# Attention, mixture of experts and gated layer in one kernel: row sums on ScalarE's accumulator, two jobs moved to GpSimd, fewer filler matmuls

## The chip, the cores and the metric

The kernel runs on one core of a Trainium2 chip. A core has five engines that run side by side and wait for each other through semaphores: TensorE (PE in the rows, with its weight loads as PEld), VectorE (DVE), ScalarE (ACT), GpSimd (POOL) and SyncE (SP), which issues most of the DMA transfers. The metric is the time of one execution in microseconds (us); lower is better.

## The reference

Three stages follow each other. The inputs q, k and v are float32 of shape (2, 8, 576, 64).

```python
# 1. attention, per batch and head, scale = 1/8, factor = 4
q_d, k_d, v_d = (mean over groups of 4 positions of q, k, v)      # 144 coarse positions
out_d = softmax(scale * q_d @ k_d.T) @ v_d, each row repeated 4 times
out_local = softmax(scale * q @ k.T where |i - j| < 4, else -1e9) @ v
x = (out_up + out_local) as 1152 tokens x 512
# each softmax: a = exp(s - max); a = a / (sum(a) + 1e-9)
# 2. experts: P from x @ w_gate by 8 rounds of row and column scaling
out = sum over e < 8 of P[:, e] * (relu(x @ w1[e]) @ w2[e])       # 512 -> 1024 -> 512
# 3. gated layer on that result: ((x @ w_a) * (x @ w_b)) @ w_out  # 512 -> 1536 -> 512
```

## The kernel before

Matrix products run on operands that are split into a high and a low part, both in a 32-bit format (fp32r in the rows): high times high, high times low and low times high are added up in PSUM. For weights the helper `split` does this: ScalarE casts the raw tile to its high part (line 134), and an engine of choice, VectorE if none is named, subtracts to get the low part (line 135).

The attention is cut into 24 items, one for each batch, pair of heads and third of the sequence (192 queries in three chunks of 64). An item goes through small stages, and the generator `side` runs them as a software pipeline: in each of its rounds `s` it issues, for five items at once, `a1` (TensorE transposes q, and k where the item is the first of its heads), `b1` (TensorE: mask, local scores, coarse scores of the item before), `c3` (ScalarE copies local weights out of PSUM), `a2` (ScalarE copies of kT and of q), `b4` (row sums, reciprocals, scaling of the exponentials), `d3` (splits the finished item into xh and xl), `b2` (VectorE: maxima), `a3` (VectorE: coarse keys and queries); then, after a yield, `d1` (TensorE: weights times v), `d2a`, `b3` (ScalarE: the exponentials), `c1` (TensorE transposes the weights), `d2`, `c2` and, for items that are the first of their heads, `sum_vd` (GpSimd sums v over groups of four, lines 865 and 868); then it yields again. "Round" below is such a pass. In the trace a round is taken from one mask matmul of `b1` to the next: 12.45, 16.64, 20.07, 24.99, 28.43, 33.40, 37.34, 42.34 and 45.85 us.

Every engine works through its own queue in the order in which the kernel is written, so that an instruction that waits holds all behind it on that engine. The order is set by hand and by the Python code that calls the generator. The main loop cuts the 1152 tokens into three blocks of 384. Ahead of block 0 it only steps through `side` until the tokens of that block are there, which takes 23 half rounds:

```python
while ready[0] < b:
    side_step()
    if b == 0:
        warm(WARM[1])
    nside += 1
    if nside > 12 and nside % 2 == 0:
        run_first(1)
```

`warm(n)` issues n bfloat16 matmuls of 256 columns whose results nobody reads; 16 more stand at the program's start. `run_first(1)` runs the next prepared weight job, here a call of `split`. Blocks 0, 1 and 2 then compute the first two halves of expert 0 (`g_plain` for the first layer, `o_moe` for the second), and between their groups of matmuls `step` goes on with the attention of the later items. From about 165 us on, the rest (experts and gated layer) runs with another order, which a planner in Python sets: the class `Model` adds up estimated times of TensorE, VectorE, ScalarE and GpSimd, and jobs are placed where these estimates let them.

What the change and the steps of the prediction touch: `queue_plain` (lines 235 to 245) prepares the first layer's weights of a unit in four pieces, i = 0, 1 and j = 0, 1, in the order (0,0), (0,1), (1,0), (1,1); j names one of two raw tiles, each of which is given back to the loading queue after its second piece. `a3` reduces the keys over groups of four (line 909), multiplies by 1/16 (line 912), and reduces the queries (line 914). `b3` takes exponentials chunk by chunk (line 950) and the coarse ones with a sum from ScalarE's accumulator (line 953). `b4` sums the local ones (line 961), adds 1e-9 (962), takes reciprocals (963), and scales the local weights on GpSimd (964) and the coarse ones on VectorE (967). The names in the rows: `p` and `pd` are local and coarse weights, `rsum` and `rr` row sums and reciprocals, `kd` coarse keys, `qdbd` coarse queries, `rv`, `rawv` and `vd` v before and after the sum over four, `pdT` and `plT` transposed weights, `raw` a raw weight tile, `w` a split one, `wz` and `identb` operands of the filler matmuls.

Of the kernel before, what the change touches and what calls it, by code (L numbers as in the profile page):

```python
# [12 lines left out]
AF = mybir.ActivationFunctionType  # L13
ALU = mybir.AluOpType
AX = mybir.AxisListType
# [4 lines left out]
def attn_moe_glu_kernel(  # L20
# [16 lines left out]
    nc = tc.nc  # L37
# [12 lines left out]
    NC = UT // 64  # L50
    W = 70
# [42 lines left out]
    def dve(us, after=None):  # L94
        M.dve = max(M.dve, M.pe if after is None else after) + us

    def act(us):
        M.act = max(M.act, M.pe) + us
# [20 lines left out]
    def new_block(uses):  # L119
        i = nring[0] % NSLOT  # L120
        assert RING[i] is None or RING[i].uses == 0
        nring[0] += 1
        t = wr.tile([128, 1024], F32R, tag=f"w{i}", name=f"w{i}")
        RING[i] = Block(t[:, 0:512], t[:, 512:1024], uses)
        return RING[i]

    def pool(us):
        M.pool = max(M.pool, M.pe) + us

    def split(b, raw, k=1, low=None):  # L130
        hi, lo = b.hi, b.lo
        if k > 1:
            hi, lo = (t.rearrange("p (k f) -> p k f", k=k) for t in (hi, lo))
        nc.scalar.copy(out=hi, in_=raw)  # L134
        (low or nc.vector).tensor_tensor(out=lo, in0=raw, in1=hi.bitcast(F32), op=ALU.subtract)  # L135
        act(0.6)
        if low is None:
            dve(0.75, 0.0)
        else:
            pool(1.35)  # L140
# [88 lines left out]
    def halves(load, left):  # L229

        rs = [Raw(lambda t, j=j: load(t, j), left[j]) for j in range(len(left))]
        lq.extend(rs)
        return rs

    def queue_plain(u, uses=6):

        u.w = {}
        rs = halves(u.load1, (2, 2))
        for i in range(2):
            for j in range(2):  # L240
                def piece(i=i, j=j):
                    b = u.w[i, j] = new_block(uses)
                    split(b, rs[j].tile[:, :, 256 * i:256 * i + 256], 2)
                    rs[j].used()
                wq.append(Task(piece, 0.68, ready=rs[j].ready, slot=True))

# [166 lines left out]
    for e in range(E):  # L413
        for hf in range(2):
            u = Unit()
# [7 lines left out]
    for g in range(GU):  # L423
        u = Unit()
# [481 lines left out]
    def a3(i, b, u, hp):  # L906
        if u == 0:
            kd_ = at.tile([128, SD], F32, tag=f"kd{hp}", name=f"kd{hp}", bufs=1)
            nc.vector.tensor_reduce(
                out=kd_, in_=kT[b, hp].rearrange("p (t r) -> p t r", r=4), axis=AX.X, op=ALU.add  # L910
            )
            nc.vector.tensor_scalar_mul(out=kd_, in0=kd_, scalar1=1.0 / 16.0)
            kd[b, hp] = kd_
        nc.vector.tensor_reduce(
            out=qdbd[i % 2].rearrange("p c h t -> p (c h t)"),
            in_=qbd[i % 2].rearrange("p c h (t r) -> p (c h t) r", r=4), axis=AX.X, op=ALU.add,
        )
# [26 lines left out]
    def b3(i, b, u, hp):  # L944
        sl, sd, nm, nd = pB[i]
        p = at.tile([128, NC, W], F32, tag="p", name="p", bufs=2)
        pd = at.tile([R, SD], F32, tag="pd", name="pd", bufs=2)
        rs = rsum[i % 4]
        for c in range(NC):
            nc.scalar.activation(  # L950
                out=p[:, c], in_=sl[:, c * W:(c + 1) * W], func=AF.Exp, bias=nm[:, c:c + 1], scale=1.0
            )
        nc.scalar.activation(
            out=pd, in_=sd, func=AF.Exp, bias=nd, scale=1.0, accum_out=rs[0:R, NC:NC + 1],
        )
        pB[i] = p, pd, rs

    def b4(i, b, u, hp):
        p, pd, rs = pB[i]
        rr = at.tile([128, NC + 1], F32, tag="rr", name="rr", bufs=2)  # L960
        nc.vector.tensor_reduce(out=rs[:, 0:NC], in_=p, axis=AX.X, op=ALU.add)
        nc.vector.tensor_scalar_add(out=rr, in0=rs, scalar1=1e-9)
        nc.vector.reciprocal(out=rr, in_=rr)  # L963
        nc.gpsimd.tensor_tensor(  # L964
            out=p, in0=p, in1=rr[:, 0:NC].unsqueeze(2).to_broadcast([128, NC, W]), op=ALU.mult
        )
        nc.vector.tensor_scalar_mul(out=pd, in0=pd, scalar1=rr[0:R, NC:NC + 1])
        pB[i] = p, pd
# [134 lines left out]
    def side():  # L1103
# [7 lines left out]
        for s in range(n + 5):  # L1111
# [14 lines left out]
            do(c3, s - 3)  # L1126
            do(a2, s)
            do(b4, s - 2)
            do(d3, s - 4)
            do(b2, s - 1)  # L1130
            do(a3, s)
            yield
            do(d1, s - 3)
            do(d2a, s - 3)
            do(b3, s - 1)
            do(c1, s - 2)
            do(d2, s - 3)
# [20 lines left out]
        )  # L1158


    WARM = (16, 3)
    SIDE = 1.25

    def warm(n):

        if n:
            ps = bank("g")
            for _ in range(n):
                mm(ps[:, :256], identb, wz, True, True)

    with tc.manual_schedule():
# [4 lines left out]
        nc.vector.memset(wz, 1.0)  # L1176
        warm(WARM[0])
        make_identity(nc, ident)
# [8 lines left out]
        for h in range(2):  # L1187
            ph = slice(64 * h, 64 * h + 64)
            for base, cm, st_ in ((9, 1, -1), (-3, -1, 1)):
                nc.gpsimd.affine_select(  # L1190
                    out=mw[ph], in_=mw[ph], compare_op=ALU.is_ge, fill=-1e30, base=base,
# [6 lines left out]


        for u in units[:2]:  # L1200
            queue_plain(u)
        for u in units[:2]:
            queue_out(u)
        queue_combined(units[2], nc.gpsimd)
# [26 lines left out]
        def close_attention():  # L1231
            nonlocal closed, ps3, Th, Tl, tmp_p
            closed = True
            attn_stack.close()
            tp = ctx.enter_context(tc.tile_pool(name="tp", bufs=1, side="right"))
            Th = tp.tile([128, 3, 2, S], F32R, name="Th")
            Tl = tp.tile([128, 3, 2, S], F32R, name="Tl")
            for x in range(3):
                G3.append([tp.tile([128, 320], F32, name=f"G{x}{fi}") for fi in range(2)])
            tmp_p = tmp_stack.enter_context(tc.tile_pool(name="tmp", bufs=1, side="right"))  # L1240
            ps3 = ctx.enter_context(tc.tile_pool(name="ps3", bufs=6, space=PSUM))
            gens[0] = gating()
            v, g = nc.vector, nc.gpsimd
            tasks = combine_x(0, lambda name: tmp_p.tile([128, 2, CN[0]], F32, name=name),
                              (v, g, g, v), (g, g, g, g))
            tq.extend(tasks)
            queue_out(units[2])
            for u in units[3:]:
                queue_combined(u)
                queue_out(u)  # L1250
            for u in glu_g:
                if u is glu_g[0]:
                    queue_plain(u, 8)
                else:
                    queue_combined(u)
                queue_out(u, 2)
            hold[0] = False
            for r in coming:
                r.tile
            fetch()  # L1260
# [36 lines left out]
        for b in range(NB):  # L1297
# [5 lines that stand above are left out]
# [155 lines left out]
```

## Time and profile before

| | us |
|---|---|
| median of three runs | 1093.15 (1090.24 to 1093.36) |
| profiled execution, whole | 1091.71 |
| profiled execution, span of its instructions | 1089.8 |
| TensorE busy in the span | 1076.0 |
| VectorE, ScalarE, GpSimd busy | 790.8, 456.8, 515.5 |

The span runs from the first to the last instruction; 1.9 us of the execution lie outside it. Times within the trace count from the span's start. Busy time counts an engine as busy from an instruction's start to its end, and the ends of matmuls are modelled. In rows of the timeline, a row gives start, duration, engine, line, operation, output and inputs, sizes, the count of merged instructions, and in brackets how long the engine sat idle before and who released it. The chain of waits is the path that ended last, followed backwards.

### The profile page before, as it was taken

The numbers are of one execution on the slowest core, as the hardware profiler recorded it, in microseconds if no ns is written. First come the engines' busy times: TensorE is split into PE (matmuls) and PEld (weight loads), VectorE is DVE, ScalarE is ACT, GpSimd is POOL, SyncE is SP. The second block draws the span as 40 slices with busy tenths as digits, with TensorE's granted clock in tenths as the row PEclk, the third lists the DMA queues.
The fourth block names the chain that finished last, engine by engine and source line by source line (L and its number), as shares of the span: only waits on it lengthen the run. The fifth ranks groups of instructions, "written<-read, shape, count | busy, mean of one in ns | idle before, by whom it ended". The sixth has DMA issues, their size and how long they took to land.

```text
span 1089.8 us, 18094 instructions
## 1 busy us (share of the span) xinstructions
PE 1076.0 (99%) x6569; PEld 974.5 (89%) x6569; DVE 790.8 (73%) x1545; ACT 456.8 (42%) x1135; POOL 515.5 (47%) x512
## 2 busy tenths in 40 slices
PE   9999999999999999999999999999999999999998
PEld 8898988999898989889898988989999899999997
DVE  7876546857887788878777888877864576677764
ACT  5664424454434443343444344344443453232221
POOL 3324116563645556464565646455561365355521
PEclk9999999999999999999999999999999999999999
DMA  7453000213323132332323233231311101111002
GB/s 173 124 144 88 22 5 17 91 47 98 102 85 103 63 124 73 113 101 85 102 64 124 62 122 101 86 102 63 110 65 49 49 1 59 58 43 56 20 21 87
DMA packets 80745, 84.52 MB, mean 78 GB/s; under 512 B 35856, under 2 KB 54288, under 8 KB 80656
## 3 DMA queue, kind: packets, MB, share of 16 engines
q1 hardware_dynamic: 79472, 83.07, 24.8%
q8 instruction: 52, 0.85, 0.3%
q10 hardware_dynamic: 1184, 0.30, 0.1%
q14 instruction: 37, 0.30, 0.1%
HBM read 71.54 MB, written 11.80 MB: 76 GB/s over the span
## 4 chain that ended last, share of the span: by engine, by line
PE 75%; DVE 13%; ACT 5%; issue 3%; DMA 2%; POOL 1%; DVEq 0%; ACTq 0%; SPq 0%; POOLq 0%
PE g L60 70%; PE at L60 3%; DVE w L135 3%; DVE G L652 2%; DVE acc L513 2%; ACT w L134 1%; ACT G L644 1%; DVE dec L374 1%; DVE dec L357 1%; DVE dec L352 1%; ACT gh L646 1%; POOL gl L648 1%; DVE gl L638 1%; DMA dec<-in_moe_w_a_dram 1%; DMA dec<-in_moe_w_b_dram 1%
## 5 line engine op out<-in xcount | busy, mean ns | idle before, releaser
L60 PE MATMUL g<-w,gh 128*128 128x512 f32 x1314 | 412.9, 395 | 0.3 <-DVE acc L513 0.3
L60 PE MATMUL g<-xh,w 128*128 128x256 f32 (+2 forms) x1536 | 339.1, 302 | 0.3 <-DVE lg L1053 0.3
L648 POOL TENSOR_TENSOR gl<-G,gh 128x256 fp32r<-128x256 f32 (+1 forms) x208 | 172.1, 836 | 269.4 <-ACT gh L646 262.9
L60 PEld LDWEIGHTS g<-w,gh 128*128 128x128 f32 x1314 | 235.7, 188 | 41.8 <-DVE acc L513 1.4
L60 PEld LDWEIGHTS g<-xh,w 128*128 128x128 f32 x1536 | 257.5, 189 | 4.7 <-DVE lg L1053 0.4
L60 PE MATMUL g<-w,gl 128*128 128x512 f32 x657 | 257.8, 392 | 0.0
L60 PE MATMUL g<-xl,w 128*128 128x320 f32 (+2 forms) x768 | 231.2, 301 | 1.5 <-POOL xl L1030 1.5
L135 DVE TENSOR_TENSOR w<-raw,w 128x512 fp32r<-128x512 f32 x139 | 137.4, 998 | 112.8 <-ACT w L134 112.6
L60 PE MATMUL g<-Th,w 128*128 128x320 f32 (+1 forms) x912 | 199.7, 295 | 1.6 <-DVE G L652 1.6
L652 DVE TENSOR_TENSOR G<-g,G 128x256 f32<-128x256 f32 (+1 forms) x380 | 154.9, 448 | 21.4 <-PE g L60 10.1
L60 PEld LDWEIGHTS g<-Th,w 128*128 128x128 f32 x912 | 152.2, 188 | 7.2 <-DVE G L652 4.3
L644 ACT ACTIVATE G<-G 128x256 f32<-128x256 f32 (+1 forms) x168 | 74.3, 443 | 192.6 <-DVE G L652 192.6
L60 PEld LDWEIGHTS g<-xl,w 128*128 128x128 f32 x768 | 145.3, 189 | 6.2 <-POOL xl L1030 2.1
L60 PEld LDWEIGHTS g<-w,gl 128*128 128x128 f32 x657 | 123.4, 188 | 28.6
L60 PE MATMUL g<-Tl,w 128*128 128x256 f32 (+1 forms) x456 | 134.0, 294 | 0.0
L134 ACT CAST w<-raw 128x512 fp32r<-128x512 f32 x180 | 107.5, 618 | 52.4 <-POOL raw L259 46.2
L646 ACT CAST gh<-G 128x256 fp32r<-128x256 f32 (+1 forms) x208 | 90.3, 434 | 92.1 <-DVE G L662 78.6
L513 DVE SCALAR_TENSOR_TENSOR acc<-g,P,acc 128x512 f32<-128x512 f32 x126 | 93.7, 744 | 47.8 <-PE g L60 44.0
L389 POOL TENSOR_TENSOR dec<-dec 128x384 f32<-128x384 f32 x48 | 48.8, 1016 | 105.5 <-DVE dec L386 59.2
L60 PEld LDWEIGHTS g<-Tl,w 128*128 128x128 f32 x456 | 85.8, 188 | 2.8
L964 POOL TENSOR_TENSOR p<-p,rr 128x210 f32<-128x210 f32 x24 | 13.2, 551 | 107.1 <-DVE rr L963 29.9
L259 POOL TENSOR_TENSOR s<-raw 128x512 f32<-128x512 f32 x38 | 61.8, 1626 | 4.3 <-DMA raw<-w 3.8
(177 smaller groups left out, 1198.3 us busy)
## 6 DMA issues: line engine op xcount, KB each, us to landing
raw<-in_moe_w_dram SPq DMA_DIRECT2D x128, 256.0 KB
w<-dec SPq DMA_DIRECT2D x48, 192.0 KB
dec<-in_moe_w_a_dram SPq DMA_DIRECT2D x16, 384.0 KB
dec<-in_moe_w_b_dram SPq DMA_DIRECT2D x16, 384.0 KB
dec<-in_moe_w_out_dram SPq DMA_DIRECT2D x16, 384.0 KB
raw<-w SPq DMA_DIRECT2D x48, 128.0 KB
raw<-w SPq DMA_DIRECT2D x12, 256.0 KB
vw<-in_v_dram SPq DMA_DIRECT2D x72, 35.0 KB
```

Source lines behind the costliest of these rows:

```text
L60: nc.tensor.matmul(out=o, lhsT=l, rhs=r, start=start, stop=stop, skip_group_check=not check)
L134: nc.scalar.copy(out=hi, in_=raw)
L135: (low or nc.vector).tensor_tensor(out=lo, in0=raw, in1=hi.bitcast(F32), op=ALU.subtract)
L259: nc.gpsimd.tensor_tensor(out=o(), in0=A(*a), in1=A(*b), op=op)
L352: nc.vector.tensor_scalar(out=m.bitcast(F32), in0=m.bitcast(F32), scalar1=2.0**-15, scalar2=122879.9921875, op0=ALU.max, op1=ALU.min,)
L389: nc.gpsimd.tensor_tensor(out=tf, in0=tf, in1=mf, op=ALU.add)
L513: nc.vector.scalar_tensor_tensor(out=a, in0=ps, scalar=P[:, tt, u.e:u.e + 1], in1=a, op0=ALU.mult, op1=ALU.add)
L644: nc.scalar.activation(out=src, in_=src, func=AF.Relu)
L646: nc.scalar.copy(out=h, in_=src)
L648: nc.gpsimd.tensor_tensor(out=l, in0=src, in1=h.bitcast(F32), op=ALU.subtract)
L652: nc.vector.tensor_tensor(out=o, in0=bank_, in1=b, op=ALU.add)
L964: nc.gpsimd.tensor_tensor(out=p, in0=p, in1=rr[:, 0:NC].unsqueeze(2).to_broadcast([128, NC, W]), op=ALU.mult)
```

## The change

The sum over the local exponentials moves from a reduction on VectorE to the accumulator output of the three exponentials on ScalarE. The multiplication of the coarse keys by 1/16 moves from VectorE to GpSimd. Of the first layer's weights of the first two units, the low parts of the pieces with j = 1 (four pieces of eight) move from VectorE to GpSimd. The second number of `WARM` goes from 3 to 1.

```diff
-    def queue_plain(u, uses=6):
+    def queue_plain(u, uses=6, low=None):
...
-                    split(b, rs[j].tile[:, :, 256 * i:256 * i + 256], 2)
+                    split(b, rs[j].tile[:, :, 256 * i:256 * i + 256], 2, low if j else None)
...
-            nc.vector.tensor_scalar_mul(out=kd_, in0=kd_, scalar1=1.0 / 16.0)
+            nc.gpsimd.tensor_scalar_mul(out=kd_, in0=kd_, scalar1=1.0 / 16.0)
...
             nc.scalar.activation(
-                out=p[:, c], in_=sl[:, c * W:(c + 1) * W], func=AF.Exp, bias=nm[:, c:c + 1], scale=1.0
+                out=p[:, c], in_=sl[:, c * W:(c + 1) * W], func=AF.Exp, bias=nm[:, c:c + 1], scale=1.0,
+                accum_out=rs[:, c:c + 1],
             )
...
-        nc.vector.tensor_reduce(out=rs[:, 0:NC], in_=p, axis=AX.X, op=ALU.add)
...
-    WARM = (16, 3)
+    WARM = (16, 1)
...
-            queue_plain(u)
+            queue_plain(u, 6, nc.gpsimd)
```

Counted over the program, VectorE has 36 instructions fewer (24 sums, 8 factors, 4 low parts), GpSimd 12 more, TensorE 46 filler matmuls with their weight loads fewer; ScalarE's 72 local exponentials get a second output; SyncE's queue is unchanged. But for these the order on every engine is the same from the first instruction to the last, also where the planner sets it.

On VectorE, in the round of 20.07 us and the start of the next, the queue before read (`kd` coarse keys, `x` the finished item, `rsum` the row sums):

```order
L909 TENSOR_REDUCE kd_452<-kT_435 128x144
L912 TENSOR_SCALAR kd_452<-kd_452 128x144
L914 TENSOR_REDUCE qdbd_113<-qbd_111 128x96
L1019 TENSOR_TENSOR x<-at,od 64x192 x2
L986 COPY pdT<-at 72x192
L961 TENSOR_REDUCE rsum_118<-p 128x3
L962 TENSOR_SCALAR rr<-rsum_118 128x4
L963 RECIPROCAL rr<-rr 128x4
L967 TENSOR_SCALAR pd<-pd,rr 96x144
```

The same stretch on VectorE with the change:

```order
L909 TENSOR_REDUCE kd_433<-kT_417 128x144
L914 TENSOR_REDUCE qdbd_113<-qbd_111 128x96
L1019 TENSOR_TENSOR x<-at,od 64x192 x2
L986 COPY pdT<-at 72x192
L962 TENSOR_SCALAR rr<-rsum_118 128x4
L963 RECIPROCAL rr<-rr 128x4
L967 TENSOR_SCALAR pd<-pd,rr 96x144
```

The factor has left the place between the two reductions, and the sum the place ahead of the reciprocals. On GpSimd, from the round of 28.43 us to that of 37.34 us, the queue before read:

```order
L865 TENSOR_TENSOR rv_415<-rv_415 72x4x128
L868 TENSOR_TENSOR vd_640<-rv_415 72x2x2x64
L964 TENSOR_TENSOR p<-p,rr 128x210
L1030 TENSOR_TENSOR xl<-x,xh 128x192
L964 TENSOR_TENSOR p<-p,rr 128x210
L1030 TENSOR_TENSOR xl<-x,xh 128x192
L865 TENSOR_TENSOR rv_569<-rv_569 72x4x128
```

The two pairs of lines 964 and 1030 belong to two rounds. With the change the same stretch on GpSimd reads:

```order
L912 TENSOR_SCALAR kd_577<-kd_577 128x144
L865 TENSOR_TENSOR rv_397<-rv_397 72x4x128
L868 TENSOR_TENSOR vd_609<-rv_397 72x2x2x64
L964 TENSOR_TENSOR p<-p,rr 128x210
L1030 TENSOR_TENSOR xl<-x,xh 128x192
L135 TENSOR_TENSOR w_679<-raw,w_679 128x512
L964 TENSOR_TENSOR p<-p,rr 128x210
L1030 TENSOR_TENSOR xl<-x,xh 128x192
L865 TENSOR_TENSOR rv_541<-rv_541 72x4x128
```

The factor now stands ahead of the sums of v, and the low part of piece (0,1) ahead of the next round's scaling of `p`.

## Rows read from the trace of the kernel before

**Rows 1.** Busy time by stretch: us, then PE, PEld, DVE, ACT, POOL.

```profile
12.45:45.85 33.40, 31.46 (x276) 28.71 (x275) 30.53 (x89) 23.81 (x91) 16.14 (x25) 1.00 0.65 166
16.64:20.07 3.43, 3.43 (x34) 3.35 (x33) 3.16 (x9) 2.51 (x10) 2.08 (x3) 1.00 0.78 217
20.07:24.99 4.92, 4.62 (x41) 3.98 (x40) 4.58 (x15) 3.20 (x14) 2.12 (x4) 1.00 0.79 167
50.20:1089.80 1039.60, 1030.56 (x6196) 934.09 (x6196) 748.42 (x1413) 424.66 (x1020) 494.99 (x473) 1.00 0.23 74
```

**Rows 2.** Chain of waits: start us, us, what.

```profile
24.16 0.33 PE g L60 x3
```

**Rows 3.** Timeline 17.8 to 22.1: start, us, engine, line.

```profile
17.84 0.55 POOL L964 TENSOR_TENSOR p<-p,rr 128x210 f32<-128x210 f32 x1 [2.76 <-PE at L60]
...
19.09 1.27 POOL L865 TENSOR_TENSOR rv<-rv 72x512 f32<-72x512 f32 x1
...
19.19 1.27 DVE L912 TENSOR_SCALAR kd<-kd 128x144 f32<-128x144 f32 x1
...
20.44 0.72 POOL L868 TENSOR_TENSOR vd<-rv 72x256 f32<-72x256 f32 x1
...
22.08 0.66 PE L60 MATMUL at<-pdT,vd 72*128 72x96 f32 x4 [0.30 <-DVE pdT L986]
```

**Rows 4.** Line 912, all eight: ns min/median/max.

```profile
L912 DVE TENSOR_SCALAR kd<-kd x8: 234/808/1295, 7.2 to 83.5; 128x144 f32<-128x144 f32 x8
```

**Rows 5.** Timeline, ACT after an exponential with a sum.

```profile
10.08 0.20 ACT L953 ACTIVATION_READ_ACCUMULATOR pd<-at,nd 96x1 f32 x1
10.17 0.40 ACT L897 COPY kT<-at 128x288 f32<-128x288 f32 x1
```

**Rows 6.** Timeline 33.6 to 36.0: first low part's round.

```profile
33.67 0.62 ACT L134 CAST w<-raw 128x512 fp32r<-128x512 f32 x1
...
34.93 0.37 DVE L961 TENSOR_REDUCE rsum<-p 128x3 f32<-128x210 f32 x1
...
35.33 0.17 DVE L962 TENSOR_SCALAR rr<-rsum 128x4 f32<-128x4 f32 x1
...
35.88 0.55 POOL L964 TENSOR_TENSOR p<-p,rr 128x210 f32<-128x210 f32 x1 [2.83 <-PE at L60]
```

**Rows 7.** Line 135 up to 180 us, on DVE and POOL.

```profile
L135 DVE TENSOR_TENSOR w<-raw,w x13: 677/692/694, 30.4 to 79.4; 128x512 fp32r<-128x512 f32 x13
...
L135 POOL TENSOR_TENSOR w<-raw,w x1: 1280/1280/1280, 176.1 to 176.1; 128x512 fp32r<-128x512 f32 x1
```

**Rows 8.** Timeline 38.2 to 39.6: DVE and POOL meeting.

```profile
38.26 0.69 DVE L135 TENSOR_TENSOR w<-raw,w 128x512 fp32r<-128x512 f32 x1 [0.24 <-ACT w L134]
38.29 1.24 POOL L868 TENSOR_TENSOR vd<-rv 72x256 f32<-72x256 f32 x1
...
39.27 0.29 DVE L962 TENSOR_SCALAR rr<-rsum 128x4 f32<-128x4 f32 x1
39.48 0.21 POOL L1155 CAST wgp<-wg 128x32 fp32r<-128x32 f32 x1
...
39.59 0.69 PE L60 MATMUL at<-pdT,vd 72*128 72x96 f32 x4 [0.76 <-POOL vd L868]
```

**Rows 9.** Timeline 28 to 33: TensorE waiting for the coarse weights.

```profile
32.25 0.36 PE L975 MATMUL at<-ident,pd 96*72 96x96 f32 x2 [0.40 <-DVE pd L967]
```

**Rows 10.** Timeline, TensorE at the start.

```profile
1.32 3.57 PE L60 MATMUL g<-wz,identb 128*128 128x256 bf16 x16 [1.32 <-DVE wz L1176]
...
4.69 0.52 PE L880 MATMUL at<-ident,qn 96*128 96x96 f32 x2
...
8.97 0.33 PE L880 MATMUL at<-ident,qn 96*128 96x96 f32 x2
```

**Rows 11.** Timeline, TensorE at the first block.

```profile
47.10 0.42 PE L60 MATMUL g<-xh,w 128*128 128x384 f32 x1
...
50.20 0.44 PE L60 MATMUL g<-xl,w 128*128 128x384 f32 x1 [1.11 <-POOL xl L1030]
```

## The prediction

> **What bounds the kernel now.** I read four views: the page's busy times, then the busy times of stretches, then the chain of waits over the first 190 us, then the timeline of the rounds. The page's 1076.0 us of TensorE in a span of 1089.8 say that little but TensorE matters for most of the program. The stretches sharpen this: from 50.20 us on TensorE is busy for 1030.56 of 1039.60 us [rows 1], and everything that the change touches beyond that point lies beside running matmuls. What can move the time are the first 47 us, ahead of block 0, whose first matmul starts at 47.10 [rows 11] and which needs what the attention's rounds compute.
>
> Take the eight rounds from 12.45 to 45.85 us. TensorE is busy for 31.46 of 33.40 us, so 1.94 us idle, and VectorE for 30.53 [rows 1]: two engines near their limit. In the round from 16.64 to 20.07 TensorE has no gap (3.43 of 3.43) [rows 1]; this is what a round costs when only TensorE's own queue counts, with two sets of three filler matmuls in it. Three of these stand in the chain with 0.33 us, 0.11 each [rows 2]. The round from 20.07 to 24.99 is longer, with 0.30 us of idle TensorE, and its story is told by VectorE and GpSimd: GpSimd starts the sum of v at 19.09 for 1.27 us; VectorE starts the factor of the coarse keys 0.10 us later, and that too takes 1.27 us and ends 0.10 us after GpSimd's instruction [rows 3]. The same instruction takes 0.234 us where it is not held, and up to 1.295 us over its eight instances [rows 4]. So VectorE is held by GpSimd there, and everything behind it with it.
>
> **Filler matmuls.** 23 places lose two matmuls each: 46 x 0.11 = 5.1 us of TensorE. They pay only where TensorE's queue is what the next stage waits for. Both of a round's places do where TensorE has no gap: 4 x 0.11 = 0.44 us. Where the round holds a wait for another engine, only the place behind that wait pays, 0.22. Of the eight rounds, I take three of the first kind (those from 12.45, 16.64, 24.99; 1.32 us) and five of the other (1.10 us). Sum 2.42; bounds 0 and 8 x 0.44 = 3.52.
>
> **Factor of the coarse keys.** Of the eight, two in the stretch are held for about 1.0 us beyond their 0.234: the one at 19.19 and, a round with keys later, the longest, 1.295 us [rows 4]. On GpSimd this hold is gone, but the saving is not 1.0, since another wait is close behind. In GpSimd's queue the factor now stands ahead of the sums of v, and TensorE needs these sums in the next round. Before, from the start of the scaling of p at 17.84 to the end of the second sum at 20.44 + 0.72 = 21.16 it took 3.32 us, and TensorE's matmul on the sum began at 22.08, 4.24 us after that start [rows 3]. GpSimd's time for the factor is not in the trace: 32 columns take it 0.21 us (line 1155) [rows 8], 256 columns with two inputs 0.72 [rows 3]; for 144 columns I take 0.45, between the two. So 3.32 + 0.45 = 3.77 instead of 4.24, a gain of 0.47 in each of the two rounds, 0.94 us in all. What is late next is thus the sum of v on GpSimd, no longer VectorE. Bounds: with 0.72 it is 0.4, with 0.21 it is 1.4. The others lie early (the first at 7.2 us) or beside the blocks' matmuls; GpSimd's longer time is hidden by the reduction of the queries on VectorE, which the coarse scores wait for as well.
>
> **Row sums.** VectorE loses line 961, 0.37 us; to the next instruction it is 0.40 (34.93 to 35.33) [rows 6]. ScalarE gains 72 reads of the accumulator. The 24 that are there already show their price: the read lasts 0.20 us, but the next instruction starts 0.09 after the read's start [rows 5]. Three a round are 0.28 us on ScalarE. Where VectorE is late, the round gains 0.40: I see this where TensorE waits 0.40 us for the scaled coarse weights at 32.25 [rows 9], and in block 0, where a first-layer matmul waits 1.11 us for a low part that stands behind the scaling of p [rows 11]. That is 0.80. Where the exponentials are late, the round loses 0.28; the chain passes through them in three rounds of the stretch, which costs 0.84. Together about nothing, with bounds of 8 x 0.28 = -2.2 and 8 x 0.40 = 3.2.
>
> **Low parts on GpSimd.** On VectorE one takes 0.69 us, on GpSimd 1.28 [rows 7]. Four move, two of them ahead of block 0. Behind one on GpSimd's queue stand the next round's scaling of p and the low part of x. For the first: ScalarE's copy ends at 33.67 + 0.62 = 34.29 [rows 6]; with 0.28 of reads ahead of it, 34.6; then 1.28 makes 35.9, and the scaling of p started at 35.88 before [rows 6]. So the 0.69 + 0.40 us that VectorE gets free in that round buy nothing: p is scaled when it was. I put this part at 0, with bounds of -1.28 and +0.69 for each of the two. The raw tile is given back later by 1.28 - 0.69 = 0.6 us, and SyncE's queue waits for that with the next load, and the loads of q and v stand behind it; since these are issued two rounds or more ahead of their use, I cost this at 0. If that cover went, it would be 0.6 us for each of the two.
>
> One collision goes: at 38.26 VectorE's subtraction starts 0.03 us ahead of GpSimd's second sum of v, which then takes 1.24 instead of 0.72 us, and TensorE waits 0.76 us for it [rows 8]. With the copy 0.28 us later on ScalarE, GpSimd comes first. This is worth up to 0.52; I take half, 0.26.
>
> **Before and after the stretch.** From 5.5 to 12.45 us one sum and one factor leave the path, and some filler: 0.3 us; from 50.20 to 165 us the few gaps of TensorE that end with an attention step may lose 0.3 us. Beyond, nothing changes.
>
> **The sum.** 2.42 + 0.94 + 0 + 0 + 0.26 + 0.6 = 4.2 us. Against the profiled execution's 1091.71 us this gives 1087.5. That execution lies between the runs shown, 1.4 us under their median of 1093.15.
>
> One rule of the Trainium skill is to be weighed here. The rows show one-source instructions of VectorE held until GpSimd's ends: line 912, and line 962 at 39.27, which takes 0.29 us instead of 0.17 and ends just behind the sum of v [rows 3, 8]. The Trainium skill's page "GPSIMD Engine Reference" (Specifications) says that GpSimd shares its SBUF interfaces with VectorE and that the two contend when a VectorE instruction runs in a 2-port mode or has two SBUF inputs; the trace agrees. By this rule the scaling of the coarse weights (line 967) would be held by a low part on GpSimd as well, which no row shows; that is the first rival below.
>
> **Rivals.**
>
> *GpSimd's low parts hold VectorE.* Line 962 is held by a running GpSimd instruction [rows 8]. If VectorE reaches lines 962 or 967 while the low part runs, it stands for up to 1.28 us, and maxima and exponentials with it. For it: both follow the coarse copy directly now, at the time at which ScalarE finishes the high part. Against it: in the first case VectorE is free for line 962 at 34.93 - 0.69 = 34.2 [rows 6], ahead of the low part at 34.6. Twice 1.28 us ahead of block 0 take 2.6 of the 4.2: 1090.1 us, no measurable change.
>
> *Everything on TensorE pays.* All 1.94 us of idle time go and all 46 filler matmuls pay 5.1 us: 1084.7. Against it: the sums of v on GpSimd, as above.
>
> *The clock falls, on the slower side.* At the start 16 filler matmuls take 3.57 us, 0.22 each, twice the later 0.11: TensorE runs at its lower level of 1.2 GHz, and after these it rises to 2.4. The same two transposes of q take 0.52 us at 4.69 and 0.33 at 8.97 [rows 10], a ratio of 1.58. If thinner filler lets the clock drop in the rounds ahead of block 0, a round of 3.43 - 0.44 = 3.0 us on TensorE becomes 4.7, while the stretch has 33.40 / 8 = 4.18 per round now. Nine such rounds cost 4.7 us, and the dense work of block 0 would first run low as the 3.57 us at the start did, at half speed, 1.8 more: 1091.71 + 6.5 = 1098.2. It decides once more than about four rounds run low, since each then loses 1.0 of what the change gives. Against it: the granted clock is 1.00 in every stretch [rows 1], and TensorE stays busy for most of each round without the filler, which is 0.6 us of 3.4. The Trainium skill's page "TensorE: Matmul & The Clock Gate" (Part 1) says that the low clock is the default state and that activity releases it, which is why this rival keeps a chance; the rows at the start agree.
>
> **How the numbers follow.** Forecast 1087.5: 0.52, its own range 1086 to 1089. GpSimd holding VectorE, or another new wait that eats most of the gain: 0.30. Everything pays: 0.06. Clock: 0.12. Within 0.3%, 3.3 us, is about what a measurement of this kernel cannot tell from no change. So faster 0.58, same 0.30, slower 0.12. The range has to hold the first three cases and the spread of the runs before, some 3 us: 1084.2 to 1092.8.
>
> **What would show it.** Right: block 0's first matmul at about 43.5 us instead of 47.10 (the sum's parts ahead of it are 3.6); line 912 on GpSimd at 0.2 to 0.7 us and no factor on VectorE held beside the sums of v; the first matmul on each sum of v now waiting for GpSimd; reads of the accumulator 0.09 us apart from what follows. Wrong: lines 962 or 967 at over 0.5 us beside line 135 on GpSimd; transposes of q at 0.52 us after 6 us; block 0 starting at 46 us or later; or a difference that arises after 165 us.

## The result: slower by 0.7%, most of it ahead of block 0

| | before | after |
|---|---|---|
| median, same chip (9 executions each) | 1093.36 us (1090.24 to 1094.05) | 1100.71 us |
| ratio after / before | | 1.007 (95%: 1.004 to 1.0099) |
| profiled execution, whole | 1091.71 | 1097.43 |
| span / mean granted clock of TensorE | 1089.8 / 1.000 | 1095.5 / 0.992 |
| TensorE, VectorE, ScalarE, GpSimd busy | 1076.0, 790.8, 456.8, 515.5 | 1077.7, 779.5, 463.0, 526.7 |
| block 0's first matmul | 47.10 | 52.36 |

The executions of the changed kernel took 1095.33 to 1109.35 us at a mean clock of 0.978 to 0.997, and one took 1759.27 us at 0.555; the ratio leaves that one out, as those below leave out one of the kernel before (2139.88 us) and two of the factor on ScalarE with one filler (1162.45 us at 0.85, and 5200.02 us). The profiled execution is the second fastest of the other eight, so its profile shows 5.7 of the 7.4 us between the medians. TensorE has 46 matmuls fewer and yet is busy 1.7 us longer: the first sign that its clock, not its work, has changed.

The span grew by 5.7 us, and block 0 starts 5.26 us later. From its first matmul to the first on `Th` (a block's work on the way to the later experts) it is 154.03 us, 152.99 before; this 1.0 us is one gap, told further below. From there to the end of the span it is 0.6 us less. So the place to look is the rounds. The busy times of stretches of the changed kernel (us, then PE, PEld, DVE, ACT, POOL, granted clock, DMA share, GB/s), cut at its own mask matmuls:

```profile
12.07:17.48 5.41, 3.87 (x37) 3.52 (x36) 4.98 (x12) 2.85 (x17) 3.04 (x4) 1.00 0.88 225
17.48:20.48 3.00, 3.00 (x30) 2.96 (x29) 2.72 (x9) 2.79 (x13) 1.14 (x2) 1.00 0.69 213
20.48:26.81 6.33, 4.77 (x37) 4.35 (x36) 5.93 (x14) 4.26 (x22) 3.61 (x5) 0.84 0.72 155
35.59:41.34 5.75, 5.75 (x30) 5.50 (x28) 3.09 (x11) 3.65 (x18) 4.40 (x6) 0.50 0.20 43
41.34:48.06 6.72, 6.72 (x36) 6.47 (x34) 4.18 (x14) 4.24 (x18) 1.44 (x5) 0.50 0.62 158
52.36:1095.50 1043.14, 1033.03 (x6209) 936.04 (x6206) 742.71 (x1401) 430.18 (x1067) 501.97 (x480) 1.00 0.24 74
```

They answer to [rows 1]. The second line is the round that was 3.43 us with TensorE always busy [rows 1]; now it takes 3.00, again without a gap. The first and the third are rounds in which TensorE needs GpSimd's sums of v: 5.41 and 6.33 us where the before's cuts gave 4.19 (12.45 to 16.64) and 4.92. The fourth and fifth took 3.94 and 5.00; TensorE is busy in all of 5.75 and 6.72 us, with fewer matmuls, at a granted clock of 0.50, its lower level of 1.2 GHz. So there are two losses: TensorE waits in the first rounds, and later it runs at half speed. These four rounds lose 1.22 + 1.41 + 1.81 + 1.72 = 6.2 us; the other four together, the time ahead of them (12.07 us instead of 12.45) and the time behind them are 0.9 us shorter, which gives block 0's 5.26.

What TensorE waits for stands in the timeline of the changed kernel:

```profile
9.11 0.19 ACT L950 ACTIVATION_READ_ACCUMULATOR p<-at,nm 128x1 f32 x1
9.20 0.31 ACT L950 ACTIVATE p<-at,nm 128x70 f32<-128x70 f32 x1
...
12.23 0.57 POOL L912 TENSOR_SCALAR kd<-kd 128x144 f32<-128x144 f32 x1 [0.85 <-DVE kd L909]
...
12.88 1.26 POOL L865 TENSOR_TENSOR rv<-rv 72x512 f32<-72x512 f32 x1
12.97 1.20 DVE L962 TENSOR_SCALAR rr<-rsum 128x4 f32<-128x4 f32 x1
...
14.22 0.72 POOL L868 TENSOR_TENSOR vd<-rv 72x256 f32<-72x256 f32 x1
14.41 1.11 DVE L967 TENSOR_SCALAR pd<-pd,rr 96x144 f32<-96x144 f32 x1
...
14.99 0.69 PE L60 MATMUL at<-pdT,vd 72*128 72x96 f32 x4 [1.54 <-POOL vd L868]
...
18.56 0.55 POOL L964 TENSOR_TENSOR p<-p,rr 128x210 f32<-128x210 f32 x1 [3.13 <-ACT kT L897]
...
19.87 0.59 POOL L1030 TENSOR_TENSOR xl<-x,xh 128x192 fp32r<-128x192 f32 x1 [0.76 <-ACT xh L1029]
...
20.54 0.57 POOL L912 TENSOR_SCALAR kd<-kd 128x144 f32<-128x144 f32 x1
...
21.19 1.26 POOL L865 TENSOR_TENSOR rv<-rv 72x512 f32<-72x512 f32 x1
...
22.53 0.73 POOL L868 TENSOR_TENSOR vd<-rv 72x256 f32<-72x256 f32 x1
...
22.73 1.67 DVE L967 TENSOR_SCALAR pd<-pd,rr 96x144 f32<-96x144 f32 x1
...
23.22 0.54 POOL L964 TENSOR_TENSOR p<-p,rr 128x210 f32<-128x210 f32 x1
...
23.32 0.69 PE L60 MATMUL at<-pdT,vd 72*128 72x96 f32 x4 [1.56 <-POOL vd L868]
...
23.72 0.59 POOL L1030 TENSOR_TENSOR xl<-x,xh 128x192 fp32r<-128x192 f32 x1
```

In the kernel before, the first of the two factors above and its sums of v:

```profile
11.51 1.26 POOL L865 TENSOR_TENSOR rv<-rv 72x512 f32<-72x512 f32 x1
...
12.34 0.53 DVE L912 TENSOR_SCALAR kd<-kd 128x144 f32<-128x144 f32 x1
...
12.85 0.73 POOL L868 TENSOR_TENSOR vd<-rv 72x256 f32<-72x256 f32 x1
```

The first two rows of the change: the accumulator is read 0.19 us long and the next exponential starts 0.09 after the read's start, as in [rows 5]. Then the factor on GpSimd: 0.57 us long, but GpSimd stood 0.85 us in front of it, waiting for VectorE's reduction of the keys. Only behind it do the two sums of v start, 0.81 us after the round's mask matmul (12.07), where before they started 0.94 ahead of it (12.45), and TensorE's matmul on them waits 1.54 us. VectorE is held in the meantime, and no longer at the factor [rows 3] but at lines 962 and 967: 1.20, 1.11 and 1.67 us where [rows 6] has 0.17 for the first and where line 967 takes 0.29 unheld (36.72, below). The hold of 1.67 outlasts the second sum, which ends at 23.26, by 1.14 us: lines 964 and 1030 on GpSimd follow without a gap, and line 967 ends behind the second of them. In the second place GpSimd waited 0.76 us for ScalarE's `xh` before `xl`; the experiments show that this wait comes with the row sums, not with the factor. From the scaling of p to TensorE's matmul on the sum it is 23.32 - 18.56 = 4.76 us; before it was 4.24 [rows 3], and forecast was 3.77.

The Trainium skill's "GPSIMD Engine Reference" (Specifications) says that GpSimd and VectorE share their SBUF interfaces; that line 967 can be held, which no row of before showed, agrees with it, at 1.67 us.

The factor's group answers to [rows 4], and the rest of the timeline to [rows 6, 10, 11]:

```profile
L912 POOL TENSOR_SCALAR kd<-kd x8: 567/568/2533, 7.1 to 87.4; 128x144 f32<-128x144 f32 x8
```

```profile
36.72 0.29 DVE L967 TENSOR_SCALAR pd<-pd,rr 96x144 f32<-96x144 f32 x1
...
36.86 1.28 POOL L135 TENSOR_TENSOR w<-raw,w 128x512 fp32r<-128x512 f32 x1 [2.10 <-ACT w L134]
...
41.02 0.53 PE L880 MATMUL at<-ident,qn 96*128 96x96 f32 x2
...
52.36 0.42 PE L60 MATMUL g<-xh,w 128*128 128x384 f32 x1
```

Seven of eight factors take 0.57 us; the eighth, 2.53, lies beside three low parts of VectorE. The first moved low part starts at 36.86, when line 967 is already running (0.29, not held). The transposes of q take 0.53 us at 41.02, the length that [rows 10] shows at the low clock. The granted clock is low from 24.73 to 28.14 and from 34.97 to 48.62 us. TensorE's gaps of 1.56 and 1.58 us at line 868 end at 23.32 and 33.30, 1.4 and 1.7 us ahead of these two falls; behind the first gap, 1.54 us up to 14.99, the clock did not fall. Before, the rounds' largest gap was 0.76 us [rows 8] and the clock stayed at 1.00.

### The profile page after: what moved, and what is told of

Its sections match the earlier page's. It is cut to its first block, busy times and chain, and to the rows that moved or that the text cites. A ratio compares the mean times of both kernels' runs of the same rounds, so it can differ in the third digit from the quotient of the medians.

```text
span 1095.5 us, 18055 instructions
## 1 busy us (share of the span) xinstructions
PE 1077.7 (98%) x6523; PEld 977.1 (89%) x6523; DVE 779.5 (71%) x1509; ACT 463.0 (42%) x1207; POOL 526.7 (48%) x524
## 4 chain that ended last, share of the span: by engine, by line
PE 71%; DVE 15%; ACT 6%; issue 4%; POOL 2%; DMA 2%; DVEq 0%; ACTq 0%; SPq 0%; POOLq 0%
PE g L60 65%; PE at L60 4%; DVE w L135 3%; DVE acc L513 2%; DVE G L652 2%; ACT G L644 2%; ACT w L134 1%; DVE dec L374 1%; DVE dec L357 1%; DVE dec L352 1%; ACT gh L646 1%; POOL gl L648 1%; DMA dec<-in_moe_w_b_dram 1%; DVE gl L638 1%; PE at L980 1%
## 5 line engine op out<-in xcount | busy, mean ns | idle before, releaser
L135 DVE TENSOR_TENSOR w<-raw,w 128x512 fp32r<-128x512 f32 x135 | 135.1, 1010 | 113.0 <-ACT w L134 112.8
L135 POOL TENSOR_TENSOR w<-raw,w 128x512 fp32r<-128x512 f32 x45 | 59.8, 1333 | 28.1 <-ACT w L134 28.1
```

## The experiments

All ratios are against the kernel before, run in turn on the same chip, with 95% intervals. The theory: GpSimd's queue, standing in front of the factor, delays the sums of v; that makes long gaps of TensorE, and with the thin filler the clock falls. The rivals: the removed filler alone does it; the row sums or low parts do.

**The change with its filler back.**

```diff
-    WARM = (16, 1)
+    WARM = (16, 3)
```

> The changed kernel with three filler matmuls a place again instead of one. Theory 1 (thin filler lets TensorE's clock fall; that is the loss): granted clock 1.000, block 0's first matmul at 45 us or earlier, 2 to 4 us faster than the kernel before, spread of the runs as narrow as before. Rival (the factor of the coarse keys on GpSimd delays the sums of v and these hold lines 962 and 967 on VectorE; the clock only follows): clock 1.000, but lines 962 and 967 still at over 0.6 us four times or more, block 0 at 48 us or later, 1 to 3 us slower than before.

Measured: 1.0013 (1.0002 to 1.0024). Line 967 is still held, 1.11 and 1.66 us, and the gaps at line 868 are 1.22, 0.70, 1.14 and 0.57 us. But the clock stays up through the rounds (this and the following stretches of experiments have the columns told above):

```profile
12.00:48.50 36.50, 32.49 (x294) 30.38 (x295) 30.91 (x82) 27.63 (x123) 21.98 (x31) 1.00 0.60 159
```

The gaps and holds thus come without the thin filler; the clock's fall ahead of block 0 does not. The eight rounds take 34.43 us, 1.03 more than before, and the first of them alone 1.22 more. Three other parts of the change are in this kernel, and it is still not faster: the outcome that was written down for the rival.

**Each part alone**, in the kernel before. The thin filler:

```diff
-    WARM = (16, 3)
+    WARM = (16, 1)
```

> The kernel before with one filler matmul a place instead of three, nothing else. Theory 1 (filler alone drops the clock): granted clock below 0.998, 4 to 8 us slower than before. Rival (the clock falls only where TensorE also has gaps of 1.5 us): clock 1.000, TensorE's gaps as before (longest ahead of 47 us 0.8), 1 to 3 us faster than before.

The factor on GpSimd:

```diff
-            nc.vector.tensor_scalar_mul(out=kd_, in0=kd_, scalar1=1.0 / 16.0)
+            nc.gpsimd.tensor_scalar_mul(out=kd_, in0=kd_, scalar1=1.0 / 16.0)
```

> The kernel before with the factor of the coarse keys on GpSimd, nothing else. If the factor's place ahead of the sums of v is the first cause: TensorE waits 1 us or more for line 868 at two or three places, lines 962 or 967 are held at over 0.6 us at two places or more, 1 to 4 us slower than before, clock 1.000 through the filler. If the factor is harmless and the clock alone the cause: 0 to 2 us faster, lines 962 and 967 at 0.17 and 0.29.

The row sums on ScalarE's accumulator:

```diff
+                accum_out=rs[:, c:c + 1],
...
-        nc.vector.tensor_reduce(out=rs[:, 0:NC], in_=p, axis=AX.X, op=ALU.add)
```

> The kernel before with the local row sums on ScalarE's accumulator, nothing else. The prediction's term: about nothing, between -3.2 and +2.2 us. If the earlier arrival of line 962 at VectorE is what brings it beside the sums of v, line 962 or 967 is held at over 0.5 us somewhere ahead of 47 us here already, and the gain stays under 1 us; if only the factor's delay of the sums does that, none is held and the gain is 1 to 3 us.

The low parts on GpSimd, with `queue_plain` as in the change:

```diff
-            queue_plain(u)
+            queue_plain(u, 6, nc.gpsimd)
```

> The kernel before with the four low parts on GpSimd, nothing else. The prediction's term: 0, between -1.4 and +2.6 us. If the low parts hold VectorE (first rival): line 962 or 967 at over 0.6 us beside line 135 on GpSimd, 1 to 3 us slower. If they only take VectorE's 0.69 us away: no such hold, block 0's first matmul 0.5 to 1.5 us earlier than 47.10.

| alone | ratio | as us |
|---|---|---|
| filler | 1.0015 (1.0000 to 1.0029) | +1.6 |
| factor | 1.0019 (1.0007 to 1.0030) | +2.1 |
| row sums | 0.9983 (0.9969 to 0.9996) | -1.9 |
| low parts | 1.0003 (0.9992 to 1.0015) | +0.3 |

(The last column is the ratio less 1, times 1092.4 us.) They add up to +2.1, against 1.007 or +7.7 for all. So something needs two parts together. The factor alone shows the mechanism of the queue in its timeline, with the clock at 1.00 in the rounds:

```profile
11.91 0.57 POOL L912 TENSOR_SCALAR kd<-kd 128x144 f32<-128x144 f32 x1 [0.85 <-DVE kd L909]
...
14.09 1.10 DVE L967 TENSOR_SCALAR pd<-pd,rr 96x144 f32<-96x144 f32 x1
...
14.67 0.69 PE L60 MATMUL at<-pdT,vd 72*128 72x96 f32 x4 [1.21 <-POOL vd L868]
```

The same 0.85 us of wait, the same hold, a gap of 1.21 us: this round takes 5.40 us instead of 4.19. The next two rounds with sums of v are shorter than before, 4.64 instead of 4.92 and 4.60 instead of 4.97, and the eight together lose 0.67 us. In the second place nothing waits for `xh` here. So not all of the +2.1 arises in the rounds; the profile has a low stretch of 3.4 us at 168.0, and 11 of its 12 executions ran at a mean clock of 0.998 or less, where 20 of 34 of the kernel before did.

The filler alone has one low stretch, and in the rounds it makes gaps of its own (one of 1.19 us at 38.8, the others up to 0.74, none longer ahead of the low stretch). Its executions take from 1091.29 to 1098.65 us, at mean clocks between 1.000 and 0.989, so that +1.6 is the middle of a wide spread:

```profile
23.20:26.60 3.40, 3.40 (x21) 3.09 (x20) 2.90 (x10) 2.75 (x10) 1.31 (x3) 0.50 0.68 154
```

The low parts alone show the first rival's mechanism, which the change itself had not shown:

```profile
34.59 1.26 POOL L135 TENSOR_TENSOR w<-raw,w 128x512 fp32r<-128x512 f32 x1 [1.32 <-ACT w L134]
...
34.81 1.07 DVE L962 TENSOR_SCALAR rr<-rsum 128x4 f32<-128x4 f32 x1
...
43.42 1.13 DVE L962 TENSOR_SCALAR rr<-rsum 128x4 f32<-128x4 f32 x1
```

Line 962 stands for 1.07 and 1.13 us beside line 135 on GpSimd, in both rounds. These two rounds take 4.10 and 3.67 us instead of 3.94 and 3.51: 0.16 more each.

The row sums alone have the wait for `xh`, and at 19 and 27 us the factor on VectorE is hardly held any more:

```profile
19.15 0.59 POOL L1030 TENSOR_TENSOR xl<-x,xh 128x192 fp32r<-128x192 f32 x1 [0.75 <-ACT xh L1029]
...
19.46 0.37 DVE L912 TENSOR_SCALAR kd<-kd 128x144 f32<-128x144 f32 x1
...
27.02 0.43 DVE L912 TENSOR_SCALAR kd<-kd 128x144 f32<-128x144 f32 x1
```

It took 1.27 us [rows 3] and 1.295 [rows 4] there. The rounds behind them become 0.81 and 1.05 us shorter (4.11 and 3.92), and the eight take 30.99 us instead of 33.40.

**Factor and filler together**, the two parts that cost something alone, and nothing else.

> The kernel before with the factor on GpSimd and one filler matmul a place, without the other two edits. If the loss is made by these two together (gaps of TensorE behind the sums of v, and too little filler to carry the clock over them): gaps of 1.2 us or more at line 868, clock at its low level for over 7 us ahead of block 0, 4 to 9 us slower than before. If the two only add up: 1.6 + 2.1, so 3 to 4.5 us slower, with one low stretch of 3.4 us at most.

Measured: 1.0073 (1.0061 to 1.0086), the whole loss of the change (+8.0 us where the two alone add to 3.7). Its stretches:

```profile
12.00:19.40 7.40, 5.86 (x37) 5.37 (x35) 5.92 (x16) 3.33 (x15) 3.04 (x4) 0.72 0.85 243
19.40:25.16 5.76, 5.76 (x31) 5.51 (x28) 2.96 (x9) 2.65 (x12) 3.24 (x5) 0.50 0.72 162
25.16:31.88 6.72, 6.72 (x37) 6.47 (x34) 3.86 (x13) 3.19 (x13) 1.57 (x3) 0.50 0.19 42
```

The clock is low from 15.3 to 32.3 us; TensorE's first matmul behind a 1.54 us gap starts at 14.93. All six executions ran at a mean clock of 0.986 to 0.992, where those of the change with its filler back had 0.996 or more. This settles which parts do it. In these traces the long falls come just after gaps of 1.5 us and more; what exactly decides whether the clock falls, the runs do not show. The factor alone had a gap of 1.21 us and kept its clock in the rounds, the change kept it behind its first gap of 1.54, the filler alone lost it behind none over 0.74, and the last experiment below lost it with three fillers. Once low, it stayed so for 17.0 us here and 13.7 in the change, with TensorE busy all the time.

**The factor on ScalarE**, where it neither holds VectorE nor stands in GpSimd's queue; row sums and low parts as in the change, three fillers.

```diff
-            nc.gpsimd.tensor_scalar_mul(out=kd_, in0=kd_, scalar1=1.0 / 16.0)
+            nc.scalar.mul(out=kd_, in_=kd_, mul=1.0 / 16.0)
```

> Sums on ScalarE's accumulator and low parts on GpSimd as in the change, three filler matmuls as before, and the factor of the coarse keys on ScalarE. If the factor's place on GpSimd ahead of the sums of v is what holds VectorE: lines 962 and 967 at 0.17 and 0.29 but for one or two, no gap over 0.8 us at line 868 ahead of 47 us, block 0's first matmul at 43 to 45 us, 2 to 4 us faster than before. If VectorE is held there wherever the factor stands: two or more holds of over 0.6 us, 0 to 1 us.

Measured: 0.9983 (0.9975 to 0.9992), 1090.35 us, level with the row sums alone. In its timeline and its rounds:

```profile
17.72 0.55 POOL L964 TENSOR_TENSOR p<-p,rr 128x210 f32<-128x210 f32 x1 [2.40 <-ACT kT L897]
...
19.34 0.32 ACT L912 ACTIVATE kd<-kd 128x144 f32<-128x144 f32 x1 [0.39 <-DVE kd L909]
...
19.58 1.27 POOL L865 TENSOR_TENSOR rv<-rv 72x512 f32<-72x512 f32 x1
...
20.93 0.74 POOL L868 TENSOR_TENSOR vd<-rv 72x256 f32<-72x256 f32 x1
...
21.29 0.41 DVE L962 TENSOR_SCALAR rr<-rsum 128x4 f32<-128x4 f32 x1 [0.21 <-ACT pd L954]
```

```profile
12.59:44.23 31.64, 30.55 (x277) 28.45 (x276) 25.36 (x77) 27.23 (x120) 18.55 (x27) 1.00 0.65 165
```

The sums of v end at 21.67, 3.95 us after the scaling of p began (4.70 with the change); line 962 is held for 0.41 us here and 0.70 in one later round, line 967 not at all. The eight rounds take 31.64 us instead of 33.40 [rows 1], and VectorE works 25.36 of them instead of 30.53. With the row sums alone they took 30.99, so that the gain is that of the row sums; the factor's place on ScalarE does no harm, and adds nothing that can be seen.

The same without the moved low parts:

```diff
-            queue_plain(u, 6, nc.gpsimd)
+            queue_plain(u)
```

> The kernel before with the sums on ScalarE's accumulator and the factor on ScalarE; low parts on VectorE, three filler matmuls. If the low parts on GpSimd are worth nothing (the prediction's term): the same as the kernel with them, within 0.5 us, 2 to 4 us faster than before. If they cost: 1 us or more faster than that kernel.

Measured: 0.9996 (0.9988 to 1.0005). Block 0 starts at 44.34 us, earlier than in any other kernel, but its profile has a low stretch at 164.9 to 168.3 us, and some 3 us are lost between block 0 and `Th` (156.04): by my estimate 1.7 for 3.4 us at half the clock, and 1.03 in a gap told in the next section. Ahead of block 0 the low parts do not help: without them the eight rounds take 31.20 us, 0.44 less. Where the 1.4 us between the two ratios come from stays open.

**The factor on ScalarE, with the low parts again, and one filler.**

```diff
-    WARM = (16, 3)
+    WARM = (16, 1)
```

> The kernel with sums and factor on ScalarE and low parts on GpSimd, and one filler matmul a place instead of three. If the clock falls because of the gaps behind the sums of v (which are gone in this kernel) and not for want of filler alone: at most one low stretch of 3.4 us, block 0 at 44 to 46 us, within 2 us of the kernel with three. If thin filler alone is enough: two low stretches or one of over 3.4 us ahead of block 0, 3 to 8 us slower than with three. If the removed filler pays as the prediction's 2.4 us: 1 to 3 us faster than with three.

Measured: 0.9992 (0.9982 to 1.0003), so no 8 us are lost where the long gaps are missing: its largest ahead of block 0 are 1.0, 0.89 and 0.79 us and its mean clock in the profile is 1.000. But less filler buys next to nothing either: the eight rounds take 31.46 us instead of 31.64, and 0.9992 is no better than 0.9983 with three.

**Filler in a later place.** Low stretches of 3.4 us also appear at 165 to 171 us. Twelve fillers at the attention's last gate scores, three a round as before, factor on ScalarE:

```diff
+                if bl == NB - 1 and kt == KT - 1:
+                    warm(5 if n % 2 == 0 else 2)
...
+        if bl == NB - 1:
+            warm(5)
```

> The same kernel with three fillers a place, and 12 filler matmuls more at the last block's gate scores (5 and 2 ahead of the last pair's products, 5 ahead of the transposes), where TensorE has gaps of 0.57, 0.23 and 0.56 us between 162 and 168 us and where three of the profiles have a low stretch of 3.4 us. If too little work in that stretch drops the clock in some executions: no low stretch there, the runs 0.5 to 1.5 us faster in the median and closer together. If the dips come without regard to it: no difference beyond 0.3 us.

Measured: 0.9983 (0.9974 to 0.9993), as without them. All 12 executions ran at 0.999 to 1.000 (3 of 11 without these fillers were at 0.998), but the time is no shorter. The fillers themselves cost nothing there: the next matmul on expert weights starts 120.14 us after block 0's, 120.18 without them. From block 0 to `Th` it is nevertheless 154.12 us instead of 153.01, through a gap of 1.02 us at 179.17 that some traces have and others do not, told in the next section.

**The factor on GpSimd, behind the sums of v**, three fillers: its wait can then delay no sum.

```diff
-            nc.gpsimd.tensor_scalar_mul(out=kd_, in0=kd_, scalar1=1.0 / 16.0)
...
+    def a4(i, b, u, hp):
+        if u == 0:
+            nc.gpsimd.tensor_scalar_mul(out=kd[b, hp], in0=kd[b, hp], scalar1=1.0 / 16.0)
...
+            do(a4, s)
```

> The changed kernel with three fillers a place and the factor still on GpSimd, but queued behind the sums of v instead of ahead of them. If the place ahead of the sums is the cause: gaps of TensorE at line 868 under 0.8 us as in the kernel before, at most one hold of line 962 or 967 over 0.6 us from lines 865 or 868, 1 us or more faster than the change with three fillers; the coarse scores may wait for the factor instead. If any factor on GpSimd costs this: gaps and holds stay, within 0.5 us of it.

Measured: 1.0014 (1.0002 to 1.0025), no faster than the change with its filler back. No hold of lines 962 and 967 is left and no gap at line 868, yet (GpSimd's factor is line 920 here):

```profile
14.04 0.64 POOL L920 TENSOR_SCALAR kd<-kd 128x144 f32<-128x144 f32 x1
...
14.73 0.49 PE L60 MATMUL at<-kd,qdbd 128*96 128x144 f32 x2 [1.01 <-POOL kd L920]
```

```profile
33.70:44.00 10.30, 10.30 (x53) 9.51 (x52) 4.41 (x14) 5.17 (x24) 4.91 (x8) 0.50 0.24 53
```

The wait moved: TensorE's coarse scores now stand 1.01, later 1.24 and 1.59 us for the factor. And behind the third of these gaps, which ends at 32.7, the clock fell for 10.3 us, with three fillers; the profiled execution has the lowest mean clock of the twelve (0.995, the others 0.996 to 0.998), so that most lost less. The filler is no sure cover, and GpSimd is a bad place for the factor on either side of the sums.

## Why the prediction was wrong, step by step

**Factor of the coarse keys: the step that failed.** It priced two rounds, "So 3.32 + 0.45 = 3.77 instead of 4.24, a gain of 0.47", and put the other factors at nothing: "The others lie early (the first at 7.2 us) or beside the blocks' matmuls". The second of the eight is neither: it started at 12.34 us, and the sums of v beside it, begun at 11.51, are those that the first of the eight rounds needs. On GpSimd it stands ahead of these sums, and the queue stands still in front of it for 0.85 us, until the keys are reduced. This round became 5.40 us with the factor alone and 5.41 in the change, instead of 4.19: a loss of 1.2 us and TensorE's first long gap, in a round that the term does not hold. In the two rounds that it does hold, the factor alone gained 0.28 and 0.37 us for the 0.47 each; its own time was 0.57 for 0.45. That in the change the priced span became 4.70 (18.56 to 23.26) and TensorE's wait with it 4.76 is mostly the 0.76 us for `xh`, which belongs to the row sums: it stands in their trace without the moved factor (0.75) and not in that of the factor alone. The 1.0 us of hold did go from line 912, but returned at lines 962 and 967, since the sums, now later, ran beside them. Priced +0.94 (least +0.4), measured alone -2.1 (-0.8 to -3.3), of which the rounds of the profile show 0.67. The prediction said that GpSimd's longer time is hidden by the reduction of the queries; what was not hidden is the wait of everything queued behind it.

**Filler matmuls.** Priced +2.42, alone -1.6 (0 to -3.2). In a round without gap the price was exact: 3.43 to 3.00, 0.43 for 0.44. Elsewhere nothing was paid. The round from 12.45, counted among those without gap, stayed at 4.18 with the filler alone. Where no clock fell (the factor on ScalarE, one filler against three) the two rounds without gap gained 0.44 and 0.43, two of those with sums of v lost 0.55 and 0.21, and all eight gained 0.18. And with the factor's gaps the thinned filler brought the low clock and some 4 us more than both alone.

**The clock falls** is the rival that came true; it had 0.12, and its 1098.2 stands close to the profiled 1097.43. "Against it" was that TensorE stays busy for most of each round. That argument took the gaps of before, where the rounds' longest was 0.76 us, for those of after: the change itself made them 1.54 to 1.58. The filler alone lost its clock once without such gaps, so the argument failed there too. Its price was nine rounds at the low clock and part of block 0; the profile has 17 us of low clock (24.73 to 28.14, 34.97 to 48.62) and the full clock in block 0, and the rest of the loss is the waits. So its number is partly luck.

**Row sums.** Priced 0 with bounds of -2.2 and +3.2; measured a gain of 1.9 (0.4 to 3.4). The read's price, 0.09, was right; of the two terms I set against each other, 0.80 and -0.84, the second is what the gain speaks against. Most of the gain, 1.86 of 2.41 us in the profile's eight rounds, arises in the two rounds behind a factor that VectorE had been held at: GpSimd, waiting for `xh`, now starts the sum of v only at 19.70, behind the factor's start at 19.46. That hold is what the factor's move was meant to remove: with the sums on the accumulator there was little of it left, 0.37 and 0.43 us. The two terms were priced as if they were independent.

**Low parts on GpSimd.** Priced 0, measured 0.3 slower (0.9 faster to 1.6 slower): right in size. In their own experiment the hold of line 962 was there and cost next to nothing, so *GpSimd's low parts hold VectorE* was right on the mechanism and wrong on its price (2.6 us).

**The collision** at 38.26 [rows 8] was to bring 0.26. With the factor on ScalarE the two still meet (line 868 takes 1.12 us) and TensorE waits 0.63 instead of 0.76: 0.13. With the row sums alone GpSimd does come first, as reckoned, and TensorE waits 0.23: 0.53, the upper bound. In the change it fell into the low clock and cannot be read.

**Before and after the stretch.** Priced +0.6; the part beyond block 0 lost 1.0 up to `Th`. It is one gap. Of the four rows on VectorE and GpSimd, the first two are from the kernel before, the others from the change:

```profile
177.49 1.83 POOL L259 TENSOR_TENSOR raw<-raw 128x512 f32<-128x512 f32 x1
177.50 0.68 DVE L599 TENSOR_TENSOR Tl<-b,Th 128x512 fp32r<-128x512 f32 x1
...
182.62 1.29 POOL L259 TENSOR_TENSOR raw<-raw 128x512 f32<-128x512 f32 x1
182.64 1.82 DVE L599 TENSOR_TENSOR Tl<-b,Th 128x512 fp32r<-128x512 f32 x1
...
185.99 0.46 PE L60 MATMUL g<-P,ones 128*128 128x90 f32 x2 [1.04 <-DVE P L1080]
```

Two instructions start within 0.02 us of each other, and in one trace GpSimd's is stretched, in the other VectorE's, and TensorE then waits 1.04 us for line 1080, which stands behind it. Up to this place the change is not late: its matmuls on `P` and `ones` begin 130.04 us after block 0's first, 130.16 before. Line 599 took 1.82 us in five of the traces, those of the change and of the last four experiments, and 0.68 in the others. So this loss hangs on which of the two goes first; how often it falls which way in one kernel, single traces do not show. A gap of 0.82 us at 84.0 is in seven of the eight kernels with the row sums on the accumulator and in none of the others; the row sums alone, which have it at 1.10, reach `Th` in 153.02 us, so that no loss is seen from it.

Of the signs named, "block 0 starting at 46 us or later" and "transposes of q at 0.52 us after 6 us" came. Holds of 962 and 967 came beside lines 865 and 868 and what follows these on GpSimd, not beside line 135, where I looked for them. A difference after 165 us came too, by the gap just told.

## What to carry to other kernels

When an instruction moves to an engine with less to do, price its place in that queue, not only its length, and do so at every place where it stands: when its input is ready there, what stands behind it meanwhile, and beside which instructions of the other engines that then runs. Here 0.57 us of work on GpSimd brought 0.85 us of standing still and 1.5 us gaps of TensorE, while ScalarE took the same step in 0.32. And where filler holds TensorE's clock, don't take it away in a change that can open gaps: the two alone cost 1.6 and 2.1 us, together 8.0.

## What the runs showed of the hardware that was not expected

- At the start TensorE works at half speed for a time that differs from trace to trace: in the change the transposes of q take 0.33 us already at 4.48, in the change with its filler back six fillers at 5.97 still take 1.41 us, where six take 0.82 at 8.53. The first mask matmul comes at 5.83 and 7.39 us with it. Profiles that differ by less than this ahead of block 0 are best compared by round, not by time.
- Low stretches of 3.4 us appear in some executions long after the rounds: at 167.6 us (the change with its filler back), at 164.9, and at 543.2 us, just behind a gap of TensorE of 1.80 us that ended at 542.47 (row sums alone).
- GpSimd and VectorE stretch each other both ways: the factor on GpSimd took 2.53 us beside three low parts of VectorE, and line 967, which reads one tile and a column of factors, took 1.67 instead of 0.29 beside the second sum of v and the two GpSimd instructions that followed it without a gap.
- A low clock did not end with work: TensorE was busy without a gap at the granted clock of 0.50 for 17.0 us (factor and filler together, 15.3 to 32.3) and 13.7 us (the change, 34.97 to 48.62).
